# The way from convolution output to channel-major activations: through TensorE, or through DRAM

## The chip, the cores and the metric

The kernel runs on one core of one Trainium2 chip. A core has five engines that work side by side and wait for each other by semaphores: TensorE (PE, matrix products, with its weight loads shown as PEld), VectorE (DVE), ScalarE (ACT), GpSimd (POOL) and SyncE (SP), which here only issues DMA transfers. The metric is the device time of one execution in microseconds, as the median over the runs shown.

## The reference

A depthwise causal convolution over time with a softmax-normalised kernel of 7 taps for each of 8 heads, and behind it a channel mix. The input is x with 8 batches, 4160 tokens and 192 channels; the hidden width is 1024.

```python
w = softmax(weight, axis=-1)                       # (8 heads, 7 taps)
y[b, s, h*24:(h+1)*24] = sum_k w[h, k] * x_pad[b, s + k, h*24:(h+1)*24]
y_prev = y shifted by one token (zero in front)
xk = mu_k * y + (1 - mu_k) * y_prev
xr = mu_r * y + (1 - mu_r) * y_prev
k = maximum(xk @ w_k, 0.0)                         # 192 -> 1024
v = (k * k) @ w_v                                  # 1024 -> 192
out = v / (1 + exp(-(xr @ w_r)))                   # 192 -> 192
```

## The kernel before

**Tiling.** Two batches are worked on together: a pair p, of which there are four. For the convolution, time is cut into blocks of BLK = 116 tokens. A block with its 6 tokens of halo in front would be 122 rows; the tile `xb` holds 128 rows of time on the partitions, for up to GB = 9 blocks, both batches of the pair and 192 channels. One matmul for each head multiplies a banded matrix `toe` (128 rows of time by BLK tokens, made from the softmaxed weights) with all blocks of a group at once (`conv_mm`, line 193). Its result lies in PSUM with tokens on the partitions. `conv_out` (lines 210 and 213) copies it to the bf16 tile `y`, so that the 384 channels of the pair form three column groups of 128.

The channel mix needs channels on the partitions. So `tr_mm` (line 226) transposes each block of `y` in three matmuls against the identity, two blocks to a PSUM tile, and `tr_out` (line 237) copies that tile to `yT`, which holds 128 channels x 3 groups x all tokens of the pair. 36 blocks a pair make four groups of nine; the first group of the first pair is split into five and four, so there are 17 groups.

Then time goes in steps of 512 tokens: `diff` (line 253) subtracts the token before, `mix` (line 275) makes `xk` and `xr`. `k_mm` (lines 308 and 312) makes one 128-wide slice of the hidden layer for both batches, `k_relu` (line 339) and `k_square` (line 353) give k squared, `v_mm` (line 388) sums over the eight slices, `r_mm` and `r_sig` (lines 369 to 378) make the gate, and `v_out` (line 400) multiplies both and sends the result out on SyncE's queue (line 405). `o_sb`, the tile that is sent, has four buffers; PSUM has two buffers each for k (`psK`), for v (`psV`) and for everything else (`psM`: convolution, transposes and gate).

**Order.** The order on each engine is written out by hand. A slot n is one `k_mm`: eight slots for a step of 512 tokens, and one more for the last 64 tokens of a pair, 65 a pair and 260 in all. Four tables (`early`, `pe`, `act`, `dve`) say which function runs in which slot, and the loop at the end runs them slot by slot: the early table, `k_mm`, the tables of ACT and PE, `k_relu`, the table of DVE, `k_square` of the slot before. The engines keep this order each for itself; no slot begins at a set time, and a load in the early table runs as soon as its buffer is free (`xb` has three).

A group whose tokens are first needed in slot n0 has its eight convolution matmuls in slots n0 - 22 to n0 - 15, each evacuated one slot later, its transposes from slot n0 - 13 on, and the step's `diff` in slot n0 - 7, with the four `mix` from n0 - 5 to n0 - 2. For the first pair's steps 1 and 2 (`late`) these are n0 - 15, n0 - 7, n0 - 4 and n0 - 3 to n0 - 1. `v_mm` runs ten slots behind `k_mm`, `v_out` every second slot, eleven behind. In numbers of lines: the tables are filled in lines 416 to 453 and run in lines 459 to 470.

Of the kernel before, what the change touches and what calls it, by code (L numbers as in the profile page):

```python
# [8 lines left out]
BF16 = mybir.dt.bfloat16  # L9
# [5 lines left out]
def kernel(  # L15
# [11 lines left out]
    nc = tc.nc  # L27

    B, S, D = x.shape
    H, K = weight.shape  # L30
    G = D // H
    DF = moe_w_k.shape[1]
    P = 128
    NF = DF // P
    LO = D - P
    HALO = K - 1
    BLK = 116
    GB = 9
    NG = 4
    STEP = 512  # L40
    NSTEP = S // STEP
    TAIL = S - NSTEP * STEP
    NPAIR = B // 2
    SPP = NSTEP * NF + 1
    NSLOT = NPAIR * SPP
    YC = 2
    LAG_V = NF + 2
    LAG_R = NF

# [1 line left out]
    two = ctx.enter_context(tc.tile_pool(name="two", bufs=2))  # L51
# [5 lines left out]
    dram = ctx.enter_context(tc.tile_pool(name="dram", bufs=1, space=bass.MemoryType.DRAM))  # L57


    groups = [  # L60
        [(g * GB, GB, 2 * g) for g in range(NG)]
        if p
        else [(0, 5, 0), (5, 4, 1)] + [(g * GB, GB, 2 * g) for g in range(1, NG)]
        for p in range(NPAIR)
    ]

# [3 lines left out]
    def load_x(p, g):  # L70
        blk0, nb, _ = groups[p][g]
        xb = three.tile([P, GB, 2, D], BF16, tag="xb", name="xb")
        xbs[p, g] = xb
        for s in range(2):
            b = 2 * p + s
            lo, hi = 0, nb
            if blk0 == 0:
                lo = 1
                nc.gpsimd.memset(xb[0:32, 0, s, :], 0.0)
                nc.gpsimd.dma_start(out=xb[HALO:P, 0, s, :], in_=x[b, 0 : P - HALO, :])  # L80
            t0 = blk0 * BLK - HALO
            if b == B - 1 and blk0 + nb == NG * GB:
                hi = nb - 1
                r0 = t0 + hi * BLK
                nc.gpsimd.memset(xb[96:P, hi, s, :], 0.0)
                nc.gpsimd.dma_start(out=xb[0 : S - r0, hi, s, :], in_=x[b, r0:S, :])
            nc.gpsimd.dma_start(  # L87
                out=xb[:, lo:hi, s, :],
                in_=bass.AP(
                    tensor=x.tensor,  # L90
                    offset=x.offset + (b * S + t0 + lo * BLK) * D,
                    ap=[[D, P], [BLK * D, hi - lo], [1, D]],
                ),
            )
# [4 lines left out]
        out=w_raw,  # L99
        in_=bass.AP(tensor=weight.tensor, offset=weight.offset, ap=[[0, P], [K, H], [1, K]]),  # L100
# [6 lines left out]
    w_row = const.tile([P, H, P], BF16)  # L107
    nc.vector.memset(w_row, 0.0)
    load_x(0, 0)
    ident = const.tile([P, P], BF16)  # L110
    nc.gpsimd.affine_select(
        out=ident,
        in_=ones_t,
# [10 lines left out]
        out=w_exp, in0=w_raw, in1=w_max.unsqueeze(2).to_broadcast([P, H, K]), op=ALU.subtract  # L124
# [6 lines left out]
        out=w_row[:, :, 0:K],  # L131
# [5 lines left out]
    nc.sync.dma_start(out=w_scr, in_=w_row)  # L137
    toe = const.tile([P, H, BLK], BF16)
    nc.sync.dma_start(
        out=toe,  # L140
        in_=bass.AP(
            tensor=w_scr.tensor,
            offset=w_scr.offset + K - 1,
            ap=[[H * P - 1, P], [P, H], [1, BLK]],
        ),
# [38 lines left out]
    ys, yTs = {}, {}  # L184
    conv_ps = {}

    def conv_mm(p, g, h):
        nb = groups[p][g][1]
        if h == 0:
            ys[p, g] = two.tile([P, GB, 2 * D], BF16, tag="y", name="y")  # L190
        ps = psM.tile([P, GB, 2, G], FP32, tag="m", name="ps_c")
        conv_ps[p, g, h] = ps
# [19 lines left out]
            n = c1 - max(c0, P)  # L212
            copy(out=yl[:, :, :, c1 - P - n : c1 - P], in_=ps[:BLK, :nb, :, G - n : G])  # L213

    tr_ps = {}

    def tr_mm(p, g, j):
        blk0, nb, _ = groups[p][g]
        if blk0 == 0 and j == 0:
            yTs[p] = two.tile([P, 3, YC + NG * GB * BLK], BF16, tag="yT", name="yT")  # L220
            nc.vector.memset(yTs[p][:, :, 0:YC], 0.0)  # L221
        ps = psM.tile([P, 3, 2, BLK], BF16, tag="m", name="ps_t")
        tr_ps[p, g, j] = ps
        for i in range(min(2, nb - 2 * j)):
            for c in range(3):
                nc.tensor.transpose(  # L226
                    out=ps[:, c, i, :],
                    in_=ys[p, g][:BLK, 2 * j + i, c * P : (c + 1) * P],
                    identity=ident[:BLK, :BLK],
                )  # L230

    def tr_out(p, g, j):
        blk0, nb, _ = groups[p][g]
        ps = tr_ps.pop((p, g, j))
        n = min(2, nb - 2 * j)
        c0 = YC + (blk0 + 2 * j) * BLK
        nc.vector.tensor_copy(  # L237
# [6 lines left out]
    def step_len(s):  # L244
        return STEP if s < NSTEP else TAIL

    def diff(p, s):
        L = step_len(s)
        c0 = YC + s * STEP
        d = two.tile([P, 3, STEP], BF16, tag="diff", name="d")  # L250
# [9 lines left out]
    def mix(p, s, i, part):  # L260

        L = step_len(s)
        c0 = YC + s * STEP - 1
        d, yT = diffs[p, s], yTs[p]
# [32 lines left out]
    def where(n):  # L297
        p, r = divmod(n, SPP)
        return p, r // NF, r % NF
# [116 lines left out]
    early, pe, act, dve = ({} for _ in range(4))  # L416

    def at(table, n, fn, *a):
        table.setdefault(n, []).append((fn, a))
# [3 lines left out]
    for p in range(NPAIR):  # L423
        for g, (blk0, nb, s0) in enumerate(groups[p]):
            n0 = p * SPP + s0 * NF
            late = p == 0 and s0 in (1, 2)
            c0, r0 = (n0 - 15, n0 - 7) if late else (n0 - 22, n0 - 13)
            if n0:
                at(early, c0 - 14, load_x, p, g)
            for h in range(H):  # L430
                at(pe, c0 + h, conv_mm, p, g, h)
                if n0 == 0 and h % 2:
                    at(dve, c0 + 1 + h, conv_out, p, g, h, nc.vector.tensor_copy)
                else:
                    at(act, c0 + 1 + h, conv_out, p, g, h, nc.scalar.copy)
            for j in range((nb + 1) // 2):
                at(pe, r0 + j, tr_mm, p, g, j)
                at(dve, r0 + 1 + j, tr_out, p, g, j)
        for s in range(NSTEP + 1):
            n0 = p * SPP + s * NF  # L440
            late = p == 0 and s in (1, 2)
            at(dve, n0 - (4 if late else 7), diff, p, s)
            for j, (i, part) in enumerate(((0, 0), (0, 1), (1, 0), (1, 1))):
                at(dve, n0 + ((-3, -2, -1, -1)[j] if late else j - 5), mix, p, s, i, part)
    for m in range(NSLOT):
        p, s, t = where(m)
# [54 lines left out]
```

## Time and profile before

| | before |
|---|---|
| median of 3 runs | 523.59 us (523.42 to 525.36) |
| the profiled execution | 521.39 us |
| its span, first to last instruction | 519.7 us |
| mean granted TensorE clock | 0.998 |
| busy: PE, PEld | 492.5, 360.1 us |
| busy: DVE, ACT, POOL | 425.3, 380.0, 51.9 us |
| DMA | 41.92 MB, mean 81 GB/s |
| instructions | 10640 |

Busy times overlap between engines, and a busy PE is modelled from the starts of its matmuls: the duration of one matmul in a group's row is longer than the distance to the next. The distance between starts on PE is therefore the better measure of what a matmul costs there. In a row of the groups stand line, engine, operation, written tile and read tiles, shapes, the count, then busy time and mean nanoseconds of one, and the idle time before with what ended it. A row of windows gives, for PE, PEld, DVE, ACT and POOL in this order, the busy time and the number of instructions in the window, then the granted clock, the DMA share and GB/s. A row of the timeline begins with the start and the duration in us. The row of a DMA queue gives packets, MB and the time of its packets as a share of what 16 DMA engines have in the span or window; that of a DMA issue gives KB each and the median us from issue to landing.

### The profile page before, as it was taken

The page shows a single profiled execution, that of the slowest core. Times are in us where ns is not written, and L with a number is a line of the kernel's source. Part 1 is how long each engine was busy: PE and PEld are TensorE (multiplying, and loading weights), DVE is VectorE, ACT ScalarE, POOL GpSimd, SP SyncE. Part 2 cuts the span into 40 slices and gives each one's busy share as a digit, 9 for nine tenths or more (in the row PEclk, how much of TensorE's full clock was granted, in tenths as well). Part 3 has the DMA queues.
Part 4 walks back from the last instruction along what each step waited for, and adds up shares of the span by engine and source line. Part 5 has one row for each costly group of instructions (what it writes and reads, how often), then busy time and mean ns, then how long its engine had stood idle before and what let it go on. Part 6 is the DMA issues. An engine that isn't in the chain of part 4 may idle for free.

```text
span 519.7 us, 10640 instructions
## 1 busy us (share of the span) xinstructions
PE 492.5 (95%) x4256; PEld 360.1 (69%) x4256; DVE 425.3 (82%) x676; ACT 380.0 (73%) x545; POOL 51.9 (10%) x74
## 2 busy tenths in 40 slices
PE   0597999999999999999999999999999999999996
PEld 0345777777777777777777777777777777777776
DVE  1498897979889797997889799797898979798862
ACT  3278768687787868778686877868687786867772
POOL 9532100001020000101002010100100000000000
PEclk9999999999999999999999999999999999999999
DMA  9986451818136181714517171451711111121113
GB/s 126 171 94 85 72 106 47 130 47 129 48 71 113 47 130 47 115 62 74 101 62 115 55 115 62 76 101 52 123 47 62 56 47 62 47 62 62 49 58 100
DMA packets 76625, 41.92 MB, mean 81 GB/s; under 512 B 42912, under 2 KB 76192, under 8 KB 76576
## 3 DMA queue, kind: packets, MB, share of 16 engines
q0 software_dynamic: 39184, 15.15, 25.7%
q1 hardware_dynamic: 37392, 26.10, 16.6%
q8 instruction: 33, 0.54, 0.4%
q14 instruction: 16, 0.13, 0.1%
HBM read 30.56 MB, written 25.82 MB: 108 GB/s over the span
## 4 chain that ended last, share of the span: by engine, by line
PE 92%; DMA 3%; DVE 2%; ACT 2%; issue 0%; DVEq 0%; SPq 0%
PE ps_v L388 33%; PE ps_k L308 21%; PE ps_k L312 21%; PE ps_c L193 4%; PE ps_t L226 4%; PE ps_r L370 4%; PE ps_r L369 4%; ACT k_sb L339 1%; DMA w_scr<-w_row 1%; DMA toe<-w_scr 1%; DVE yT L237 1%; DMA w_raw<-in_weight_dram 1%; DVE xk L275 1%; DVE d L253 0%; PE ps_k L326 0%
## 5 line engine op out<-in xcount | busy, mean ns | idle before, releaser
L339 ACT ACTIVATE k_sb<-ps_k 128x1024 bf16<-128x1024 f32 x260 | 266.6, 1025 | 108.2 <-PE ps_k L312 105.8
L388 PE MATMUL ps_v<-wv,k 128*128 128x192 bf16 x2048 | 210.9, 246 | 0.0
L388 PEld LDWEIGHTS <-k 128*128 128x128 bf16 x2048 | 173.5, 98 | 35.6 <-issue 2.2
L353 DVE TENSOR_TENSOR k<-k_sb 128x1024 bf16<-128x1024 bf16 x256 | 175.0, 684 | 24.2 <-ACT k_sb L339 22.6
L308 PE MATMUL ps_k<-xk,wk 128*128 128x512 bf16 x512 | 153.1, 381 | 1.8 <-DVE xk L275 1.4
L312 PE MATMUL ps_k<-xk,wk 128*128 128x512 bf16 x512 | 153.2, 381 | 0.0
L400 DVE TENSOR_TENSOR o_sb<-ps_v,r_sb 128x384 f32<-128x384 f32 x132 | 72.4, 548 | 39.6 <-PE ps_v L388 35.6
L312 PEld LDWEIGHTS <-wk 128*128 128x128 bf16 x512 | 50.3, 98 | 61.1 <-issue 0.8
L378 ACT ACTIVATE r_sb<-ps_r 128x384 bf16<-128x384 f32 x132 | 65.0, 492 | 8.1 <-PE ps_r L370 5.0
L275 DVE SCALAR_TENSOR_TENSOR xk<-d,mu,yT 128x1024 bf16<-128x1024 bf16 x64 | 65.5, 1024 | 0.6
L193 PE MATMUL ps_c<-xb,toe 128*116 128x432 bf16 (+2 forms) x136 | 46.6, 346 | 20.0 <-DMA toe<-w_scr 16.4
L275 DVE SCALAR_TENSOR_TENSOR xr<-d,mu,yT 128x1024 bf16<-128x1024 bf16 x64 | 64.7, 1015 | 0.9
L369 PE MATMUL ps_r<-wr,xr 128*128 128x192 bf16 x256 | 63.0, 246 | 0.6 <-ACT y L213 0.6
L370 PE MATMUL ps_r<-wr,xr 128*128 128x192 bf16 x256 | 63.0, 246 | 0.0
L210 ACT CAST y<-ps_c 116x432 bf16<-116x432 f32 (+4 forms) x99 | 45.5, 460 | 16.3 <-PE ps_c L193 16.0
L87 POOL DMA_DIRECT2D xb<-in_x_dram x34 | 32.2, 950 | 247.3 <-PE ps_c L193 218.4
L308 PEld LDWEIGHTS <-wk 128*128 128x128 bf16 x512 | 46.4, 98 | 3.9 <-issue 2.9
L226 PEld LDWEIGHTS <-y 116*128 116x128 bf16 x432 | 30.1, 99 | 20.4 <-issue 1.2
L237 DVE COPY yT<-ps_t 128x696 bf16<-128x696 bf16 (+1 forms) x80 | 38.3, 479 | 4.7 <-PE ps_t L226 3.8
L193 PEld LDWEIGHTS <-toe 128*116 128x116 bf16 x136 | 18.6, 138 | 32.4 <-DMA toe<-w_scr 16.4
L226 PE MATMUL ps_t<-ident,y 116*128 116x116 bf16 x432 | 35.9, 217 | 0.5 <-DVE yT L221 0.3
L253 DVE TENSOR_TENSOR d<-yT 128x1536 bf16<-128x1536 bf16 (+1 forms) x36 | 32.0, 889 | 0.1
(55 smaller groups left out, 135.9 us busy)
## 6 DMA issues: line engine op xcount, KB each, us to landing
out_dram<-o_sb SPq DMA_DIRECT2D x128, 192.0 KB, 2.0
xb<-in_x_dram POOLq DMA_DIRECT2D x23, 432.0 KB, 7.7
xb<-in_x_dram POOLq DMA_DIRECT2D x7, 384.0 KB, 5.7
xb<-in_x_dram POOLq DMA_DIRECT2D x4, 192.0 KB, 4.6
wv<-in_moe_w_v_dram POOLq DMA_DIRECT2D x1, 384.0 KB, 6.5
out_dram<-o_sb SPq DMA_DIRECT2D x8, 48.0 KB, 2.0
xb<-in_x_dram POOLq DMA_DIRECT2D x8, 45.8 KB, 3.8
wk<-in_moe_w_k_dram POOLq DMA_DIRECT2D x1, 256.0 KB, 5.5
```

The source lines that it names most:

```text
L193: nc.tensor.matmul(out=ps[:BLK, :nb], lhsT=toe[:, h, :], rhs=xbs[p, g][:, :nb, :, h * G : (h + 1) * G], start=True, stop=True,)
L226: nc.tensor.transpose(out=ps[:, c, i, :], in_=ys[p, g][:BLK, 2 * j + i, c * P : (c + 1) * P], identity=ident[:BLK, :BLK],)
L275: nc.vector.scalar_tensor_tensor(out=o, in0=d[r0:r1, sl, :L], scalar=mu[r0:r1, i, part : part + 1], in1=yT[r0:r1, sl, c0 : c0 + L], op0=AL ...
L308: nc.tensor.matmul(out=ps[:, i, :], lhsT=wk[:, 0, fs], rhs=xk[:, i, :], start=True, stop=False)
L312: nc.tensor.matmul(out=ps[:, i, :], lhsT=wk[:, 1 + i, fs], rhs=xk[:, 2, :], start=False, stop=True)
L339: nc.scalar.activation(out=k_sb, in_=ps.rearrange("p a b -> p (a b)"), func=AF.Relu)
L353: nc.vector.tensor_tensor(out=o, in0=k_sb, in1=k_sb, op=ALU.mult)
L369: nc.tensor.matmul(out=o, lhsT=hi, rhs=wr[:, 0, :], start=True, stop=False)
L370: nc.tensor.matmul(out=o, lhsT=lo, rhs=wlo, start=False, stop=True)
L378: nc.scalar.activation(out=r_sb[:, :n, :], in_=ps[:, :n, :], func=AF.Sigmoid)
L388: nc.tensor.matmul(out=o, lhsT=k2[:, f, t * P : (t + 1) * P], rhs=wv[:, f, :], start=(f == 0), stop=(f == NF - 1),)
L400: nc.vector.tensor_tensor(out=o_sb[:, :n, :], in0=v_ps.pop(m)[:, :n, :], in1=r_sbs.pop(m)[:, :n, :], op=ALU.mult)
```

## The change

`y` no longer goes through TensorE, except for the two groups that feed the first two steps of the first pair. `y_write` sends a group of `y` to a DRAM tensor `y_dram` with tokens as rows of 384 channels, and `y_read` brings the same rows back into `yT` by a transposing DMA. Both are issued by SyncE, and the read waits for the write. Blocks have 112 tokens, 38 of them a pair, in groups of 10, 10, 9 and 9 (5, 5, 10, 9 and 9 for the first pair); the tile `yT` begins its tokens at column 16 instead of 2. The convolution of a group that goes through DRAM starts two slots earlier; `y_write` stands in the slot of its last evacuation, `y_read` two slots later. The last block of each batch is now loaded by itself, since it is not full.

```diff
-    BLK = 116
-    GB = 9
-    NG = 4
+    BLK = 112
+    GB = 10
+    NBLK = -(-S // BLK)
...
-    YC = 2
+    YC = 16
...
     groups = [
-        [(g * GB, GB, 2 * g) for g in range(NG)]
+        [(0, 10, 0), (10, 10, 2), (20, 9, 4), (29, 9, 6)]
         if p
-        else [(0, 5, 0), (5, 4, 1)] + [(g * GB, GB, 2 * g) for g in range(1, NG)]
+        else [(0, 5, 0), (5, 5, 1), (10, 10, 2), (20, 9, 4), (29, 9, 6)]
         for p in range(NPAIR)
     ]
...
-            if b == B - 1 and blk0 + nb == NG * GB:
+            if blk0 + nb == NBLK:
                 hi = nb - 1
                 r0 = t0 + hi * BLK
-                nc.gpsimd.memset(xb[96:P, hi, s, :], 0.0)
+                nc.gpsimd.memset(xb[:, hi, s, :], 0.0)
...
+    def new_yT(p):
+        yTs[p] = two.tile([P, 3, YC + NBLK * BLK], BF16, tag="yT", name="yT")
+        y_drams[p] = dram.tile([NBLK * BLK, 2 * D], BF16, tag=f"y{p % 2}", name="y_dram")
+        nc.vector.memset(yTs[p][:, :, 0:YC], 0.0)
+
+    def y_write(p, g):
+        blk0, nb, _ = groups[p][g]
+        if blk0 == 0:
+            new_yT(p)
+        nc.sync.dma_start(
+            out=y_drams[p][blk0 * BLK : (blk0 + nb) * BLK, :].rearrange("(n t) c -> t n c", t=BLK),
+            in_=ys[p, g][:BLK, :nb, :],
+        )
+
+    def y_read(p, g):
+        blk0, nb, _ = groups[p][g]
+        r0, r1 = blk0 * BLK, (blk0 + nb) * BLK
+        nc.sync.dma_start_transpose(
+            out=yTs[p][:, :, YC + r0 : YC + r1], in_=y_drams[p][r0:r1, :]
+        )
...
+            on_pe = p == 0 and s0 < 2
             late = p == 0 and s0 in (1, 2)
             c0, r0 = (n0 - 15, n0 - 7) if late else (n0 - 22, n0 - 13)
+            if not on_pe:
+                c0 -= 2
...
-            for j in range((nb + 1) // 2):
-                at(pe, r0 + j, tr_mm, p, g, j)
-                at(dve, r0 + 1 + j, tr_out, p, g, j)
+            if on_pe:
+                for j in range((nb + 1) // 2):
+                    at(pe, r0 + j, tr_mm, p, g, j)
+                    at(dve, r0 + 1 + j, tr_out, p, g, j)
+            else:
+                at(dve, c0 + H, y_write, p, g)
+                at(dve, c0 + H + 2, y_read, p, g)
```

More of the change, by code (lines that the diff above doesn't have):

```diff
@@ L213, in conv_out @@
             copy(out=yl[:, :, :, c1 - P - n : c1 - P], in_=ps[:BLK, :nb, :, G - n : G])
-    tr_ps = {}
+    tr_ps, y_drams = {}, {}
+    def new_yT(p):
[16 more added lines that the diff above has]
+        )
     def tr_mm(p, g, j):
@@ L219, in tr_mm @@
         if blk0 == 0 and j == 0:
-            yTs[p] = two.tile([P, 3, YC + NG * GB * BLK], BF16, tag="yT", name="yT")
-            nc.vector.memset(yTs[p][:, :, 0:YC], 0.0)
+            new_yT(p)
         ps = psM.tile([P, 3, 2, BLK], BF16, tag="m", name="ps_t")
```

## The prediction

> **What bounds the kernel now.** I read the page first, for its busy shares and its chain of work that ended last, then the same chain by line with decimals.
>
> ```profile
> span 519.7 us, 10640 instructions
> ...
> PE 92%; DMA 3%; DVE 2%; ACT 2%; issue 0%; DVEq 0%; SPq 0%
> ```
>
> ```profile
> by line: PE ps_v L388 32.9%; PE ps_k L308 20.7%; PE ps_k L312 20.7%; PE ps_c L193 4.4%; PE ps_t L226 4.2%; PE ps_r L370 4.1%; PE ps_r L369 4.1%; ACT k_sb L339 1.2%; DMA w_scr<-w_row 1.1%; DMA toe<-w_scr 0.8%; DVE yT L237 0.7%; DMA w_raw<-in
> ```
>
> TensorE carries 92% of the chain. The transposes (ps_t) hold 4.2% of 519.7, 21.8 us, and their evacuation to yT only 0.7%. But a busy PE is modelled, so I checked it in two more views: the windows of the middle of the run, and the timeline, where the first matmul of line 308 marks the start of each slot.
>
> ```profile
> 100.00:200.00 100.00, 100.00 (x878) 73.77 (x877) 86.86 (x140) 76.82 (x110) 7.33 (x10) 1.00 0.42 82
> 200.00:300.00 100.00, 100.00 (x873) 73.52 (x871) 85.84 (x138) 78.22 (x116) 7.32 (x10) 1.00 0.41 80
> ```
>
> ```profile
> 159.01 0.59 PE L308 MATMUL ps_k<-xk,wk 128*128 128x512 bf16 x2
> ...
> 161.00 0.59 PE L308 MATMUL ps_k<-xk,wk 128*128 128x512 bf16 x2
> ...
> 162.85 0.59 PE L308 MATMUL ps_k<-xk,wk 128*128 128x512 bf16 x2
> ...
> 164.54 0.59 PE L308 MATMUL ps_k<-xk,wk 128*128 128x512 bf16 x2
> ...
> 168.09 0.59 PE L308 MATMUL ps_k<-xk,wk 128*128 128x512 bf16 x2
> ...
> 169.97 0.59 PE L308 MATMUL ps_k<-xk,wk 128*128 128x512 bf16 x2
> ```
>
> In each 100 us PE is busy for 100, DVE (third pair) for 86 to 87, ACT for 77 to 78, and the granted clock is 1.00. The slots differ by what PE does in them: 1.99 us with six transposes, 1.85 with three, 1.69 with neither transposes nor convolution, 1.88 with one convolution matmul. So PE is the bound from slot to slot, and what is taken off it there shortens the run.
>
> **The change, part by part.** First what leaves PE. Six transposes cost 1.99 - 1.69 = 0.30 us, three cost 0.16. A group of nine blocks has four full slots and a half one: 4 x 0.30 + 0.16 = 1.36 us. Fifteen of the 17 groups lose them; the two first ones of the first pair keep 30 transposes (27 before). So 402 of 432 go. By slots, 14 groups of the steady part give 14 x 1.36 = 19.0 us; by the chain, 21.8 / 432 = 50.5 ns, 14 x 27 give 19.1. I take 19.1 and treat the fifteenth group, at the start, by itself.
>
> What PE gains: 38 blocks a pair instead of 36, so 2 x 48 columns x 8 heads = 768 more columns of convolution a pair, 3072 in all. A 432-column matmul costs 1.88 - 1.69 = 0.19 us, 0.44 ns a column: **+1.4 us**. The number of convolution matmuls stays 136.
>
> The other engines, from the groups with shapes kept apart:
>
> ```profile
> L339 ACT ACTIVATE k_sb<-ps_k 128x1024 bf16<-128x1024 f32 x260 | 266.6, 1025 | 108.2 <-PE ps_k L312 105.8 <-PE ps_k L326 0.3
> ...
> L378 ACT ACTIVATE r_sb<-ps_r 128x384 bf16<-128x384 f32 x128 | 63.7, 497 | 7.9 <-PE ps_r L370 4.8
> ...
> L210 ACT CAST y<-ps_c 116x432 bf16<-116x432 f32 x75 | 38.5, 514 | 0.5 <-PE ps_c L193 0.5
> ...
> L237 DVE COPY yT<-ps_t 128x696 bf16<-128x696 bf16 x64 | 33.0, 516 | 4.5 <-PE ps_t L226 3.8
> ```
>
> DVE loses 74 of its 80 copies, at most 74 x 0.516 = 38 us. It was not the bound, so I count nothing for them. ACT's evacuations grow from 432 to 480 columns in the groups of ten: 514 ns scaled whole is 571. A slot with convolution then has 1.025 + 0.497 / 2 + 0.571 = 1.84 us of ACT, against 1.88 + 0.02 of PE. That stays under PE, and ACT has slack in the eight slots without convolution, so again nothing. If that cover failed, each of the 0.01 us by which ACT went over would cost 8 x 15 x 0.01 = 1.2 us.
>
> What is added is a way through memory: a write of y to DRAM on SyncE's queue, a wait for its landing, and a transposing read on the same queue. It costs no compute engine anything; what matters is whether it lands before the subtraction of line 253 wants it. The time for that, from the last evacuation of a group to its first subtraction:
>
> ```profile
> 151.44 0.51 ACT L213 CAST y<-ps_c 116x432 bf16<-116x432 f32 x1
> ...
> 163.73 0.95 DVE L253 TENSOR_TENSOR d<-yT 128x1536 bf16<-128x1536 bf16 x1
> ```
>
> 151.95 to 163.73 is 11.8 us; less the transposes (1.36), plus the two slots by which the change starts the convolution earlier (2 x 1.69), **13.8 us**. If DVE then waits, its v_out waits behind, and PE goes on until psV's two buffers are full, some three slots later: 3 x 1.75, about 5 us. So PE feels nothing until **19 us** after y is ready.
>
> What the way takes, from the DMA rows, the whole run first and then the window of 12 to 20 us, in which the toe load is all that the hardware queue moves:
>
> ```profile
> q0 software_dynamic: 39184, 15.15, 25.7%
> q1 hardware_dynamic: 37392, 26.10, 16.6%
> ...
> out_dram<-o_sb SPq DMA_DIRECT2D x128, 192.0 KB, 2.0
> ```
>
> ```profile
> q1 hardware_dynamic: 1040, 0.24, 15.4%
> ...
> toe<-w_scr SPq DMA_DIRECT2D x1, 232.0 KB, 4.2
> ```
>
> ```profile
> 180.83 1.98 POOL L87 DMA_DIRECT2D xb<-in_x_dram  x2 [25.87 <-PE ps_c L193]
> 211.05 1.97 POOL L87 DMA_DIRECT2D xb<-in_x_dram  x2 [28.25 <-PE ps_c L193]
> ```
>
> The write is 1120 rows of 768 bytes. A packet of q1 takes 0.166 x 519.7 x 16 / 37392 = 36.9 ns of an engine, so 70 on each of 16 engines take 2.6 us; an output write (256 rows) has 0.6 us of packets in its 2.0, so 1.4 is latency, and the write alone is 4.0 us. It isn't alone: the load of x is released by the last convolution matmul of a group (the rows of POOL), thus at the same moment. Its 2560 packets at 0.257 x 519.7 x 16 / 39184 = 54.5 ns hold the engines for 8.7 us. One packet of it between any two of the write gives 70 x 91.4 + 1.4 = 7.8 us. I take 6, between 4.0 and 7.8.
>
> The read has no row. Counted as rows of 256 bytes (1120 x 3 column groups), the nearest one is the toe load, short runs from DRAM on the same queue: 0.154 x 8 x 16 / 1040 = 18.9 ns a packet. So 3360 / 16 x 18.9 = 4.0 us, with the toe's remaining 3.0 us of its 4.2 as latency: 7 us. Lower than that only if rows are moved in larger pieces: 2.6 us of packets and 1.4 of latency, as for the write, 4.0. From above: if every 16 rows land as 128 pieces of 32 bytes, 26,880 pieces at the same 18.9 ns are 31.8 us and 35 with latency. Between the ends I take the toe row and let the rest of the x load add 3 us: 10. Write and read together: **16 us**, between 8 and 43. That is 2 us late for the subtraction and 3 us early for PE, so the sum takes 0 for it.
>
> The Trainium skill, page DMA: Bandwidth & Descriptors, section Latency and other measured facts, gives a transposing DMA 261 GB/s in one measured kernel; an estimate from it is 860 KB in 3.3 us, which would leave the sum the same, and no transposing DMA runs in this trace to test it.
>
> SyncE's queue: the read is issued two slots after the write and holds the queue until the write has landed, 6 - 3.4 = 2.6 us. Behind it stand only output writes, and these then stand behind the read's packets, 4 to 7 us. An output write comes every second slot and o_sb has four buffers, so one may be 8 x 1.69 - 2.0 = 11.5 us late before v_out waits. 2.6 + 7 = 9.6 is under that, but not by much. POOL's order keeps its loads; a group of ten only loads 11% more. The change of alignment (YC) moves no instruction.
>
> The start: in the group for steps 2 and 3 of the first pair the read is issued only three slots before the subtraction.
>
> ```profile
> 43.44 0.34 PE L193 MATMUL ps_c<-xb,toe 128*116 128x432 bf16 x1 [0.61 <-DVE yT L237]
> ...
> 46.39 0.34 PE L193 MATMUL ps_c<-xb,toe 128*116 128x432 bf16 x1 [0.61 <-DVE yT L237]
> ```
>
> These slots now last 46.39 - 43.44 = 2.95 us, with transposes, convolution and waits for the psM copies. Without them they could take the 1.88 of a slot with convolution: four such slots, -4 us. Against it, y is ready about slot 7 and PE runs dry about slot 14, seven slots of 1.69 or 12 us later, and the way takes 16: +4 us. Bounds -4 (all of it hidden) to +27 (43 - 12 - 4); I take the two together as 0.
>
> **Sum:** -19.1 + 1.4 + 0 = -17.7 us. The profiled execution took 521.39 us around its span of 519.7; 521.39 - 17.7 = 503.7. The median of the runs shown is 523.59, 2.2 above it, so I forecast **506 us** as the median.
>
> **The rivals.**
> 1. *Slower: the transposing read is late for every group.* The place is the subtraction at line 253 waiting for the DMA, DVE in order behind it, then PE without psV buffers. It decides from a read of 19 - 6 = 13 us; each us over it costs 15 us in the run. At 20 us, between my 10 and the upper end of 35, that is 15 x 7 = 105 us: 611 us; at 35 us, 836. For it speaks that no row shows a transposing DMA and that the bounds are far apart; against it, that a read as slow as the toe row leaves 3 us. By the Trainium skill, page Advanced Engine Details and Errata, section DGE: Hardware vs Software, transposes go worse through the hardware queue than through the software one; the page has no figure and the trace no such DMA, so it bears on this rival without a price.
> 2. *The read is a little late*, 13.2 to 14 us: 3 to 15 us given back, 509 to 521.
> 3. *Output writes behind the read become the wait.* SyncE is held, o_sb's four buffers fill, and v_out stops. It decides at 11.5 us of delay. With the write at its upper 7.8 and the read at 10, the delay is 4.4 + 10 = 14.4: 3 us over, of which some 2 reach PE, 15 x 2 = 30 us: 536. Against it: output writes come only every 3.4 us.
> 4. *PE was not the bound, or ACT takes over in the slots with convolution.* Then nothing is gained: 523. The slot lengths speak against it.
>
> **How the numbers follow.** Forecast (499 to 510, the start and the small unknowns between -7 and +4): 0.67. Rival 2: 0.08, nearly all of it still faster. Rival 3: 0.05; rival 4: 0.03; rival 1: 0.17. A difference under 0.5%, 2.6 us, is about what a measurement of this kernel can tell from no change. Faster: 0.67 + 0.07 = 0.74. Same: 0.01 of rival 2, 0.01 of rival 3 and the 0.03 of rival 4, 0.05. Slower: 0.21. The range for 8 in 10 has to reach past rivals 2 and 4 into rival 3: **498 to 535**. The forecast's own range is 499 to 510.
>
> **What would show it.** Right: slots without convolution at 1.69 us where they were 1.99; 30 transposes and 6 copies left; PE still busy for 100 of 100 us in the middle; DVE near 79 of 100; read landing within 13 us; no wait of line 253 for a DMA beyond 5 us. Wrong: idle time of DVE before line 253 put down to the transposing read; PE idle before ps_v; SyncE's waits for o_sb turned into DVE waiting for output writes. The number is wrong first if the read's time is, and next if the start of the first pair is.

## The result, and the profile after

The changed kernel takes 505.98 us as the median of 4 runs (505.30 to 506.86), against 523.50 us for the kernel before beside it (523.03 to 525.36): a ratio of 0.966, 95% interval 0.9632 to 0.9688. It is faster, by what was forecast (506 us). The profiled execution took 506.09 us. Ratios here and below leave out two executions that ran slow as a whole: one of 728.85 us at a mean granted clock of 0.668, of the kernel with the read four slots later, and one of 519.07 us, of the kernel with everything earlier.

The page of the changed kernel, its span, the busy times and the chain by engine:

```profile
span 504.4 us, 9713 instructions
...
PE 472.2 (94%) x3791; PEld 340.2 (67%) x3854; DVE 390.7 (77%) x602; ACT 378.1 (75%) x545; POOL 57.8 (11%) x88
...
PE 89%; DMA 6%; DVE 2%; ACT 1%; issue 1%; DVEq 0%; SPq 0%
```

TensorE still carries the end. (63 of its matmuls are missing from this profile: one line has 449 where the program has 512, so 472.2 us is a little low.) VectorE is down by 35 us of busy time, and transfers have doubled their share of the chain, from 3% to 6%. The starts of a slot in the middle of the run and of the next one, from the timeline of TensorE, and the waits (us in all, how often, the longest):

```profile
157.46 0.59 PE L330 MATMUL ps_k<-xk,wk 128*128 128x512 bf16 x2
...
159.15 0.59 PE L330 MATMUL ps_k<-xk,wk 128*128 128x512 bf16 x2
```

```profile
DVE d L275 <- DMA yT<-y_dram: 24.4, 12, 7.5
...
PE ps_v L410 <- DVE o_sb L422: 3.3, 1, 3.3
```

The slot that had six transposes lasts 1.69 us now, as those without any did before. VectorE does wait for the transposing read, in 12 of 15 groups, but TensorE idles for it only once, 3.3 us, behind the longest wait, that of the first pair's third group. The other 14 groups are called the steady groups below. So eleven waits, 24.4 - 7.5 = 16.9 us in all, cost TensorE nothing.

Where did the time go? The starts of two kinds of matmul cut each run into three stretches: from the first convolution matmul to the first pair's tail step, from there to the last pair's tail step (the steady part), and from there to the end. Their rows, before and after (min, median and max duration, then first and last start):

```profile
L319 PE MATMUL ps_k<-tail,wk x32: 219/219/219, 145.7 to 506.3; 128*128 128x128 bf16 x32
...
L193 PE MATMUL ps_c<-xb,toe x136: 316/346/453, 16.4 to 452.5; 128*116 128x432 bf16 x120, 128*116 128x240 bf16 x8, 128*116 128x192 bf16 x8
```

```profile
L341 PE MATMUL ps_k<-tail,wk x32: 219/219/219, 145.4 to 491.0; 128*128 128x128 bf16 x32
...
L193 PE MATMUL ps_c<-xb,toe x136: 343/359/607, 16.8 to 435.2; 128*112 128x432 bf16 x64, 128*112 128x480 bf16 x56, 128*112 128x240 bf16 x16
```

The steady part went from 360.6 to 345.6 us, the stretch of the start from 129.3 to 128.6, and the end from 13.4 to 13.4. The gain is all in the steady part, 15.0 us; in the start, where three ordinary groups also lost their transposes, almost nothing is left of it.

These stretches are needed for what follows too, because the first convolution matmul itself begins at another time from profile to profile, 16.3 to 22.7 us: it waits for the first transfers from DRAM, in all profiles but one for the load of `toe`, which landed after 4.2 us in the changed kernel and after 9.7 in the run with everything earlier. Two profiles of the changed kernel have 16.8 and 16.9; whether the program or the single execution sets the time, no run shows. So a few us between two total times can lie in this opening alone, and the stretches behind it are the better measure.

### The profile page after: what moved, and what is told of

Read it like the earlier page. It is cut to its first block, busy times and chain, and to the rows that moved or that the text cites. A ratio compares the mean times of both kernels' runs of the same rounds, so it can differ in the third digit from the quotient of the medians.

```text
span 504.4 us, 9713 instructions
## 1 busy us (share of the span) xinstructions
PE 472.2 (94%) x3791; PEld 340.2 (67%) x3854; DVE 390.7 (77%) x602; ACT 378.1 (75%) x545; POOL 57.8 (11%) x88
## 4 chain that ended last, share of the span: by engine, by line
PE 89%; DMA 6%; DVE 2%; ACT 1%; issue 1%; DVEq 0%; SPq 0%
PE ps_v L410 34%; PE ps_k L334 23%; PE ps_k L330 19%; PE ps_c L193 5%; PE ps_r L392 4%; PE ps_r L391 4%; DMA y_dram<-y 2%; DMA w_scr<-w_row 1%; DMA yT<-y_dram 1%; DMA toe<-w_scr 1%; DMA w_raw<-in_weight_dram 1%; ACT k_sb L361 1%; DVE d L275 1%; ACT y L210 0%; DVE xk L297 0%
## 5 line engine op out<-in xcount | busy, mean ns | idle before, releaser
L410 PEld LDWEIGHTS <-k 128*128 128x128 bf16 x2048 | 177.0, 98 | 55.8 <-issue 4.3
L334 PE MATMUL ps_k<-xk,wk 128*128 128x512 bf16 x512 | 153.5, 382 | 3.1
L330 PE MATMUL ps_k<-xk,wk 128*128 128x512 bf16 x449 | 140.0, 382 | 1.5 <-DVE xk L297 0.7
L193 PE MATMUL ps_c<-xb,toe 128*112 128x432 bf16 (+2 forms) x136 | 48.4, 361 | 18.9 <-DMA toe<-w_scr 16.8
L210 ACT CAST y<-ps_c 112x432 bf16<-112x432 f32 (+5 forms) x99 | 47.2, 478 | 16.3 <-PE ps_c L193 16.0
L275 DVE TENSOR_TENSOR d<-yT 128x1536 bf16<-128x1536 bf16 (+1 forms) x36 | 32.4, 901 | 24.4 <-DMA yT<-y_dram 24.4
L193 PEld LDWEIGHTS <-toe 128*112 128x112 bf16 x136 | 18.6, 138 | 33.7 <-DMA toe<-w_scr 16.8
L392 PEld LDWEIGHTS <-xr 128*128 128x128 bf16 x256 | 25.1, 98 | 1.1 <-issue 0.9
L391 PEld LDWEIGHTS <-xr 128*128 128x128 bf16 x256 | 25.1, 98 | 0.6 <-issue 0.5
L213 ACT CAST y<-ps_c 112x432 bf16<-112x432 f32 (+5 forms) x49 | 23.8, 485 | 0.5 <-PE ps_c L193 0.4
```

The costliest lines, as they stand in the source:

```text
L193: nc.tensor.matmul(out=ps[:BLK, :nb], lhsT=toe[:, h, :], rhs=xbs[p, g][:, :nb, :, h * G : (h + 1) * G], start=True, stop=True,)
L210: copy(out=yh[:, :, :, c0 : c0 + n], in_=ps[:BLK, :nb, :, 0:n])
L330: nc.tensor.matmul(out=ps[:, i, :], lhsT=wk[:, 0, fs], rhs=xk[:, i, :], start=True, stop=False)
L334: nc.tensor.matmul(out=ps[:, i, :], lhsT=wk[:, 1 + i, fs], rhs=xk[:, 2, :], start=False, stop=True)
L391: nc.tensor.matmul(out=o, lhsT=hi, rhs=wr[:, 0, :], start=True, stop=False)
L392: nc.tensor.matmul(out=o, lhsT=lo, rhs=wlo, start=False, stop=True)
```

## The experiments

The theory: TensorE's time decides, and the way through DRAM is hidden except in the first pair's third group. The rivals: VectorE's relief brings the gain; the new blocks do; the waits that VectorE still has cost something after all.

**Blocks of 112 alone.** All groups stay on TensorE:

```diff
-            on_pe = p == 0 and s0 < 2
+            on_pe = True
```

> Blocks of 112 tokens in groups of ten and nine, but all transposes on TensorE and all copies to yT on VectorE, at the slots of before; nothing goes through DRAM. Theory (TensorE time decides): 3072 more columns of convolution cost 1.4 us and 456 instead of 432 transposes 1.2 us, so about 2.5 us slower than before, 526 us. Rival (the new blocking itself brings the gain, by its alignment or its groups): 506 to 515 us.

Measured 523.93 us, ratio to before 1.002 (0.9987 to 1.0054); steady part 361.5 us, 0.9 more than before. The blocks bring no gain.

**TensorE's work back.** The transposes run again beside the way through DRAM, into PSUM that nobody reads:

```diff
-    def tr_mm(p, g, j):
+    def tr_mm(p, g, j, alone=False):
...
-        if blk0 == 0 and j == 0:
+        if blk0 == 0 and j == 0 and not alone:
...
                 at(dve, c0 + H + 2, y_read, p, g)
+                for j in range((nb + 1) // 2):
+                    at(pe, r0 + j, tr_mm, p, g, j, True)
```

> The changed kernel, and TensorE does the removed transposes as well, into a PSUM tile that nobody reads (426 more transposes, no copies); yT still comes through DRAM, so the extra transposes do not reach the output. Theory (TensorE time decides): 14 steady groups give back 19 us or a little more for the ten-block groups, 525 us. Rival (the relief of VectorE brings the gain): 506 to 509 us.

Measured 526.33 us, ratio to before 1.0068 (1.0038 to 1.0097). The whole gain is gone, though VectorE has all its relief:

```profile
L341 PE MATMUL ps_k<-tail,wk x32: 219/219/219, 149.4 to 510.6; 128*128 128x128 bf16 x32
```

The steady part is 361.2 us, 15.6 more than in the changed kernel, for the 11 groups whose transposes fall into it: 1.42 us a group.

**VectorE's work back.** A multiply on a scratch tile stands wherever a copy was removed:

```diff
+    junk = const.tile([P, 2, 768], BF16, tag="junk", name="junk")
...
+    def dve_work():
+        nc.vector.tensor_tensor(out=junk[:, 1, :], in0=junk[:, 0, :], in1=junk[:, 0, :], op=ALU.mult)
...
                 at(dve, c0 + H + 2, y_read, p, g)
+                for j in range((nb + 1) // 2):
+                    at(dve, r0 + 1 + j, dve_work)
```

> The changed kernel, and VectorE does a multiply of about half a microsecond on a scratch tile wherever a copy to yT was removed (71 of them, about 37 us of VectorE). Theory (VectorE has room): 506 us, at most 4 us more where a late subtraction leaves it less room. Rival (the relief of VectorE brings the gain): most of the 17 us come back, 518 to 523 us.

Measured 508.97 us, ratio 0.9725 (0.9679 to 0.9771). VectorE is busy for 422.4 us, so 31.7 of its 34.6 us are back (75 multiplies where 74 copies were saved), and nearly all of the gain stays. The steady part is 348.0 us, 2.4 more, and the waits say why:

```profile
PE ps_v L416 <- DVE o_sb L428: 5.8, 4, 3.5
```

TensorE now idles four times for VectorE instead of once. The room is there, but not much of it.

**The read later.** SyncE gets the transposing read of the 14 steady groups four or six slots later:

```diff
-                at(dve, c0 + H + 2, y_read, p, g)
+                at(dve, c0 + H + (2 if p == 0 and s0 == 2 else 6), y_read, p, g)
```

(with 8 in place of 6 for the later one).

> The changed kernel with the transposing read four slots later in SyncE's order for the 14 steady groups (six slots behind the write instead of two). SyncE already waits for the write until about 9 us after it, so the read comes only 1 to 2 us later. Theory (TensorE does not feel the read until about 5 us after VectorE wants it): VectorE waits 2 us longer per group and the time stays at 506 us, at most 509. Rival (the reserve is already used up): 15 to 28 us more, 521 to 534 us.

> The same with the read six slots later, thus about 5 us later than now. Theory: VectorE waits about 6.5 us per group, 1 to 2 us over the reserve of 5, and 14 groups make 14 to 28 us of it: 520 to 534 us, with TensorE idle before ps_v. Rival (TensorE has a much larger reserve, the buffers in front of it hide the whole wait): 506 us.

The first took 511.88 us, the median of three executions, with a ratio of 0.9805 (0.9719 to 0.9891) and a steady part of 350.9 us, 5.3 more; the second 519.94 us, 0.9926 (0.9888 to 0.9965) and 357.5 us, 11.9 more. The expectation for four slots, no more than 509, was wrong: the reserve is smaller than 5 us. For six slots the time came out at the lower end of the 520 to 534 expected, with both terms too high: VectorE waits 3.6 us a steady group, not 6.5, and TensorE idles 9 us behind these waits. The timelines of VectorE and TensorE in the run with four slots show how large it is (the bracket is the idle time before, and what ended it):

```profile
166.02 0.96 DVE L275 TENSOR_TENSOR d<-yT 128x1536 bf16<-128x1536 bf16 x1 [3.60 <-DMA yT<-y_dram]
...
285.91 0.96 DVE L275 TENSOR_TENSOR d<-yT 128x1536 bf16<-128x1536 bf16 x1 [5.53 <-DMA yT<-y_dram]
```

```profile
167.51 0.82 PE L410 MATMUL ps_v<-wv,k 128*128 128x192 bf16 x8 [1.26 <-DVE o_sb L422]
...
282.18 0.82 PE L410 MATMUL ps_v<-wv,k2t 128*128 128x192 bf16 x8
...
287.39 0.82 PE L410 MATMUL ps_v<-wv,k 128*128 128x192 bf16 x8 [3.18 <-DVE o_sb L422]
```

3.60 - 1.26 = 2.34 and 5.53 - 3.18 = 2.35: in these groups, the second ones of the second and third pair, TensorE stalls for all that VectorE waits beyond 2.35 us; the run with six slots gives 2.34 and 2.35 for such groups too. In other groups a wait of 3.46 us passed unseen, and one of 4.20 cost 0.38. So the reserve is 2.3 to 4 us. In the second groups the `v_mm` of the tail step (`k2t`) stands shortly before the stall and takes one of psV's two buffers for a single `v_mm` instead of two; that this makes their reserve smaller is argued, no run tests it. The changed kernel runs at the edge: its longest steady wait, 2.52 us, lies in a first group, but the second group of the third pair waits 2.25, a tenth of a microsecond under its reserve. With VectorE's work back such groups stall already from 1.40 and 1.20 us on (2.54 - 1.14 and 2.11 - 0.91), so VectorE's relief isn't the gain, but it widens the reserve by about 1 us.

**Everything earlier.** The convolution, write and read of the steady groups start six slots ahead of the old place:

```diff
-                c0 -= 2
+                c0 -= 2 if late else 6
```

> The changed kernel with the convolution, the write and the read of the 14 steady groups four slots earlier (six before the old place instead of two). Theory (the waits of VectorE for the read in the steady part are hidden from TensorE): the waits at the subtraction fall from 24 us in all to the 7.5 of the start, and the time stays within 1 us of 506. Rival (these waits cost TensorE something): the time falls by several us, to 495 to 502.

The steady part is 345.3 us, within 0.3 of the changed kernel's, and VectorE waits for no read there. So the steady waits of the changed kernel cost TensorE nothing. But the time was 514.16 us, ratio 0.9796 (0.9725 to 0.9867), not within 1 us of 506 as expected. What is longer lies in the opening and the start (the profiled execution is its longest, 519.07 us, so their sizes are not read off). Its timeline of SyncE and its waits:

```profile
52.66 5.98 SPq L235 DMA_TRANSPOSE yT<-y_dram  x1
58.75 0.53 SPq L227 DMA_DIRECT2D y_dram<-y  x1
```

```profile
DVE d L275 <- DMA yT<-y_dram: 13.8, 1, 13.8
...
PE ps_v L410 <- DVE o_sb L422: 10.1, 1, 10.1
```

In the start the read of the third group now runs beside a load of x, issued at 53.80 us, and the write of the fourth, and the one wait left is 13.8 us instead of 7.5.

**The start on TensorE.** The third group is transposed there as before:

```diff
-            on_pe = p == 0 and s0 < 2
+            on_pe = p == 0 and s0 <= 2
```

> The changed kernel with the group for steps 2 and 3 of the first pair also transposed on TensorE, in the slots of before; its 14 other groups go through DRAM. Theory (the start loses because that one group's way through DRAM ends after VectorE wants it): up to the first pair's tail step the start of before took 145.7 us, and 3.7 us of that go with the three other groups, so 142.0 against 145.4 now, that is 502.6 us. Rival (the start loses by larger blocks and larger loads): 506 us or more, since 30 transposes come back.

Measured 509.74 us, ratio 0.974 (0.9679 to 0.9801), where 502.6 were expected. The stretch of the start is 127.6 us, 1.0 shorter than in the changed kernel where 3.4 were expected. The waits of the convolution for the copies of psM return (0.6 us a slot), so taking this group off the slow way gains little. The rest of the miss is no matter of the start: the opening is 2.5 us longer, and the steady part 1.9, of which TensorE idles 1.71 behind one wait of 4.05 us.

**The start earlier.** The third group's convolution and write begin two more slots ahead:

```diff
-                c0 -= 2
+                c0 -= 4 if late else 2
```

> The changed kernel with the convolution and the way through DRAM of the first pair's third group two slots earlier still, the other groups as they are. Theory (the start loses 3.3 us of idle TensorE and some more at a lower clock because this read lands late): y is ready about 2.7 us earlier, and the run is 2 to 4 us shorter, 502 to 504. Rival (the earlier convolution delays the first k matmul as much as it gains): 506.

Measured 512.46 us, ratio 0.9781 (0.9731 to 0.9831); the stretch of the start is 129.1 us, not shorter at all, and the expected 502 to 504 were missed (the opening alone is 4.9 us longer). From SyncE's timeline and VectorE's:

```profile
41.60 0.35 SPq L227 DMA_DIRECT2D y_dram<-y  x1
47.12 8.53 SPq L235 DMA_TRANSPOSE yT<-y_dram  x1
```

```profile
58.33 0.96 DVE L275 TENSOR_TENSOR d<-yT 128x1536 bf16<-128x1536 bf16 x1 [7.61 <-DMA yT<-y_dram]
```

For comparison the same stretch in the changed kernel's chain (start and duration):

```profile
39.69 8.36 DMA y_dram<-y
...
48.06 6.12 DMA yT<-y_dram
```

The write is issued 3.0 us earlier, counted from the first convolution matmul, and lands after 5.5 us instead of 8.4, but the read takes 58.33 - 47.12 = 11.2 instead of 6.1. From 46 to 52 us the queue of the loads fills the DMA engines (117 to 142% of their time in windows of 2 us; packet times overlap), and the read's queue gets 15% at most. What the one transfer gains by leaving the load of x behind, the other loses by running into it. The theory as it stood ("y is ready too late") fell here; that the load of x sets the end is tested next.

**Loads behind the read.** So the load that takes over a group's buffer is held until that group's read has landed, by a copy of one column on GpSimd:

```diff
+    order = [(p, g) for p in range(NPAIR) for g in range(len(groups[p]))]
+    gate = const.tile([P, 1], BF16, tag="gate", name="gate")
...
+        k = order.index((p, g)) - 3
+        if k > 1:
+            q, b0, n = order[k][0], *groups[order[k][0]][order[k][1]][:2]
+            c = YC + (b0 + n) * BLK - 1
+            nc.gpsimd.tensor_copy(out=gate, in_=yTs[q][:, 0, c : c + 1])
         xb = three.tile([P, GB, 2, D], BF16, tag="xb", name="xb")
```

Beside it on one chip ran the changed kernel itself, and the same without any load of x behind the third.

> The changed kernel as it is, as the measure for the other runs beside it: 506 us, and between the first and the last pair's tail step 345.6 us, as in its profile.

> The changed kernel, and GpSimd copies one column of yT, the last one that the transposing read of the same group's way writes, before it issues the load of x that takes over that group's buffer; so the load runs behind the write and the read instead of beside them. Theory (the way through DRAM is slow because it shares the 16 DMA engines with the load): the write lands in 4 to 5 us instead of 6.6 to 8.3, the read is issued 2 to 4 us earlier, VectorE's waits at the subtraction fall from 24 us in all to under 8, nearly all of it at the start, where TensorE idles 3.3 us less and the clock does not fall: 3 to 5 us shorter than the changed kernel beside it, while the stretch between the tail steps stays within 1 us of it. Rival (write and read are slow by themselves): the waits stay and the time too. Rival (loads that come some 15 us later delay the convolution): longer.

> The changed kernel without the loads of x behind the third one: all later groups convolve the third group's tokens, so most of the output is not the reference's. It measures write and read with no load beside them. Theory (the load beside them is what makes the way long): write 4.0 us, as worked out from the output writes, read 5 us, 9 us together instead of 15; no wait of VectorE for the read in the steady part. Rival (they are slow by themselves): 6.6 to 8.3 and 6.7 us as in the changed kernel.

The changed kernel took 508.18 us there, ratio 0.9709 (0.9682 to 0.9736); with loads held back it is **501.12 us, ratio 0.9594 (0.9540 to 0.9647)**, the fastest version of all, 7 us better than the changed kernel beside it, where 3 to 5 were expected. Without the loads the only execution took 503.36 us, with an opening 2.1 us longer and stretches of 122.3 and 345.6, no better than with loads held back. The DMA issues (KB each, median us to landing), first of the changed kernel in its own profile, then with loads held back, then without loads:

```profile
y_dram<-y SPq DMA_DIRECT2D x8, 756.0 KB, 8.3
y_dram<-y SPq DMA_DIRECT2D x7, 840.0 KB, 6.6
...
yT<-y_dram SPq DMA_TRANSPOSE x15, 6.7
```

```profile
y_dram<-y SPq DMA_DIRECT2D x8, 756.0 KB, 4.7
y_dram<-y SPq DMA_DIRECT2D x7, 840.0 KB, 5.0
...
yT<-y_dram SPq DMA_TRANSPOSE x15, 5.3
```

```profile
y_dram<-y SPq DMA_DIRECT2D x8, 756.0 KB, 4.7
y_dram<-y SPq DMA_DIRECT2D x7, 840.0 KB, 5.0
...
yT<-y_dram SPq DMA_TRANSPOSE x15, 5.4
```

Held back, the transfers are as short as with no load at all. The one wait of VectorE that is left, and no wait of TensorE for v_out any more:

```profile
DVE d L282 <- DMA yT<-y_dram: 3.6, 1, 3.6
```

The steady part is 345.6 us, the same as in the changed kernel's own profile and 1.1 less than in the run beside it, where one wait of 3.31 us had cost 0.96. The stretch of the start is 122.7 us instead of 128.6 and 129.6. That is where the version gains.

How can an idle time of 3.3 us cost 6? The windows of the start in the changed kernel (the number after the five engines is the granted clock), and then those with loads held back:

```profile
52.00:54.00 2.00, 0.38 (x2) 0.10 (x1) 0.00 (x0) 1.67 (x3) 0.00 (x0) 1.00 1.08 244
54.00:56.00 2.00, 0.31 (x3) 0.29 (x3) 1.79 (x3) 0.00 (x0) 0.00 (x0) 0.84 0.01 4
56.00:58.00 2.00, 2.00 (x12) 1.44 (x10) 2.00 (x4) 0.00 (x0) 0.00 (x0) 0.50 0.31 98
58.00:60.00 2.00, 2.00 (x15) 1.38 (x14) 2.00 (x5) 0.94 (x2) 0.49 (x1) 0.81 0.00 0
```

```profile
54.00:56.00 2.00, 2.00 (x17) 1.44 (x16) 2.00 (x5) 1.56 (x4) 1.70 (x3) 1.00 0.84 66
56.00:58.00 2.00, 2.00 (x17) 1.32 (x16) 2.00 (x3) 1.52 (x3) 0.07 (x1) 1.00 1.56 175
```

After the idle time TensorE is granted half its clock for some microseconds: (1 - 0.50) x 2 + (1 - 0.81) x 2 = 1.4 us lost in the two windows in which it is busy throughout. With 3.3 of idle time that is some 5 of the 6 us. In the changed kernel's run beside it the clock is 0.50, 0.50 and 0.65 in the three windows from 56 to 62 us, 2.7 us lost, and with 3.3 of idle time that is 6 of 6.9. The rest is not traced.

## Why the prediction was right, point by point

**The bound and the removed work.** Right. The transposes were priced at 1.36 us a group of nine by the slots; the run that puts them back costs 1.42 a group, with groups of ten among them. The steady part lost 15.0 us; the forecast has 11 x 1.36 for its groups less about 0.7 us of convolution columns, 14.3.

**Nothing for VectorE and ACT.** Right: giving VectorE its work back, 422.4 us busy, cost only 2.4 us of the steady part. For ACT no run varied anything; TensorE waits 2.1 us for it in the changed kernel's list of waits, against 1.6 before.

**The way through DRAM, 16 us.** Right in the sum, mis-sized in its terms: the write was put at 6 and took 6.6 to 8.3, the read at 10 and took 6.7. Alone they take 4.7 to 5.0 and 5.4, where 4.0 and 7 were worked out. With the loads held back, the first read of the run moves 3392 packets, 3360 of them the predicted rows of 256 bytes, which hold the 16 engines for 71.3% of 5.9 us, 4.2 us where the toe load's price gave 4.0. So the count and the price of the packets were right; too dear was the toe's 3.0 us of latency, since 5.7 us to landing leave 1.5 beside the packets. The 3 us added to the read for the load of x, and the write's 2 us, fell the other way round: the write is the one that the load delays most. The page DMA: Bandwidth & Descriptors of the Trainium skill, section Latency and other measured facts, gives a transposing DMA 261 GB/s in one kernel, by which an estimate is 860 KB in 3.3 us. In the window of that first read its 0.87 MB pass within some 3.8 us (26 of the 40 slices of the window's 5.9 us), by estimate 230 GB/s, which is near it; the landing after 5.7 us includes more than that.

**Two us late for VectorE, three early for TensorE.** The first holds: 16.9 us of waits in eleven steady groups, 1.5 each. The second was the step with the weakest footing. The reserve behind VectorE was counted as three slots, 5 us; the runs with a later read show 2.3 to 4. The forecast held because the read is as early as it is: in the repeat of the same kernel one wait came out at 3.31 us, and TensorE idled 0.96.

**The start, taken as 0.** Mis-sized, and inside its bounds of -4 to +27. Three ordinary groups saved 3 x 1.36 less 0.5 of convolution there, 3.6 us, and the stretch became 0.7 shorter: +2.9 for the third group. Both of its terms were off. By the starts of `k_mm`, counted from the first convolution matmul, slot 14 comes 34.4 us in instead of 36.1, so the slots without transposes brought 1.7 us and not 4. Slots 14 and 15 then last 8.7 us instead of 3.8, so the late read cost 4.9 and not 4: the idle time of 3.3, and the lower clock behind it, which was not foreseen at all.

**The number.** Partly luck. From profiled execution to profiled execution the change is 521.39 - 506.09 = 15.3 us where 17.7 were forecast. The 2.2 us that the forecast added, since the median of before lay above its profiled execution, aren't there in the changed kernel, whose median and profiled execution agree within 0.1; the two errors cancel.

**The rivals.** The slow read (1) did not come: it takes 6.7 us, not the 13 at which it was to decide, though with the reserve that the runs show it would have decided 1 to 3 us sooner. The Trainium skill, page Advanced Engine Details and Errata, section DGE: Hardware vs Software, has transposes fare worse by the hardware queue than by the software one. No run here sends one through the software queue, so that stays untested; alone, the read lands after 5.4 us, a plain write of the same bytes by the same queue after 4.7 to 5.0. The little delay (2) is what the runs with a later read produced on purpose. Output writes behind the read (3) land in 2.3 us in the median instead of 2.0, and VectorE never waited for their buffers. But SyncE stood longer before the reads than the 2.6 us worked out, 6.0 on average (us in all, how often, the longest):

```profile
SPq L235 <- DMA y_dram<-y: 89.7, 15, 8.4
```

That TensorE was not the bound (4) is excluded by the run that puts its work back.

**Its own signs.** The slot of 1.69 us, the 30 transposes and the 6 copies are there; VectorE is busy for 82 of 100 us in the middle of the run, where 79 were expected. One sign of being right is not: line 253's wait (line 275 now) was to stay under 5 us and reached 7.5 in the start. Two signs of being wrong are there in small, VectorE's idle time before that line and one idle time of TensorE before ps_v; the latter lies in the start, so the steady part lost nothing by them.

## What to carry to other kernels

Before work is moved from a busy engine to transfers, add up what else the DMA engines do at that moment: here the load released by the last matmul of a group ran beside the new write and read, and the two took 13 to 15 us instead of 10. If such a load isn't urgent, hold it until the urgent transfer has landed. And price a late operand by the buffers that really lie between it and the bound engine: here a wait was free up to that reserve and cost one for one beyond it.

## What the runs showed of the hardware that was not expected

- A transposing read holds the queue that issues it. In the changed kernel's list of SyncE's instructions:

```profile
L235 SPq DMA_TRANSPOSE yT<-y_dram x15: 2943/4197/7402, 48.1 to 441.6; - x15
```

 SyncE needs 2.9 to 7.4 us to issue one, against about 0.37 us for an output write; without loads beside it, still 3.1 to 5.1 us.
- The clock fell to 0.50 after 3.3 us of idle TensorE in the start, and so it did after 3.3 to 3.6 us there in five other profiles, but in the run with the read six slots later an idle time of 3.42 us at about 296 us left it at 1.00. The Trainium skill, page TensorE: Matmul & The Clock Gate, Part 1, has a window of about 3.4 us that runs freely, and throttles after an idle one. By that, an idle time of just that length may go either way; why it fell every time in the start and not at 296 us, no run here shows.
- The first transfers from DRAM end at very different times: the first convolution matmul began between 16.3 and 22.7 us in profiles of nearly the same opening, and with it the whole run shifts.
